# Expert 0's up weights in two column halves with products by contraction, and the remainder's values one group later

## The chip, the cores and the metric

The kernel runs on one core of a Trainium2 chip. The metric is the device time of one launch in microseconds; most launches of this kernel fall between 533.9 and 535.5 us, so that differences under about 1 us can't be read from single times.

## The reference, cut to what matters

Eight batches of retention (causal attention with decay instead of softmax) feed a mixture of four experts that all run on every token.

```
scores = scale * q @ k^T;  ret = scores * Dmat (causal decay)
x      = (ret @ v) as [4608 tokens, 512]
p      = domain_probs / sum(domain_probs)
out    = sum over e of p[:, e] * (relu(x @ w1[e]) @ w2[e])      # w1 512 x 1024, w2 1024 x 512, e = 0..3
```

## The kernel before

One batch has 576 rows: four chunks of 128 and a remainder of 64. Experts work on tiles of 512 tokens. Tile 0 is batch 0's chunks; while its expert products run, the remainder of batch 0 and all of batch 1 are computed in between. The products are cut into *groups* (8 matmuls of 512 columns each for tile 0), and after group n the helper `run(slots, n)` emits whatever was added to slot n. In the traces here, every engine runs its instructions in the order in which they were emitted.

All accumulators of TensorE lie in PSUM and come from one ring of four buffers of two banks each. A new accumulator inherits the buffer of an earlier one, and its first matmul waits until that one has been read.

```python
def load_w1(e, f=slice(0, F)):                      # GpSimd's queue, float32 -> bf16 on the way
    return nc.gpsimd.dma_start(out=w1_sb[e][:, :, f], in_=moe_w1[e][:, f].rearrange("(dc p) f -> p dc f", p=128))

class UpHalf:                                       # expert 0, 512 columns, 256 tokens
    def matmuls(self, i):
        for fc in range(2 * i, 2 * i + 2):          # column block by column block
            for dc in range(NDC):                   # contraction innermost
                nc.tensor.matmul(self.ph[:, fc, :], lhsT=w1_sb[0][:, dc, fc * 128:(fc + 1) * 128],
                                 rhs=xt_of(0)[:, dc, self.c], start=(dc == 0), stop=(dc == NDC - 1))
# ... cuts ...
class Rem:                                          # the remainder of one batch
    def scores(self):
        # ... 4 matmuls into sr ...
        nc.vector.tensor_tensor(self.sT, s, trir[:, :].unsqueeze(1).to_broadcast([128, NP, R]), op=MULT)
    def values(self):
        o = ring_tile("or", [128, NP, R])           # 8 matmuls, 4 of which read sT
# ... cuts ...
load_w1_at = {1: (slice(0, F // 4),), 2: (slice(F // 4, F // 2), slice(F // 2, 3 * F // 4)),
              3: (slice(3 * F // 4, F),)}
# ... cuts ...
for at, f in ((11, lambda: rem0.cast(nc.vector)), (11, rem0.trans_dma), (19, rem0.scores), (20, rem0.values)):
    add(at, f)
for u, (c, tr, sc, o) in enumerate(((18, 21, 22, 23), (20, 22, 24, 25), (24, 0, 28, 29), (25, 0, 29, 30))):
    add(c, lambda u=u: v_cast(u))                   # batch 1: k, q cast on VectorE, v on GpSimd
    if u < 2:
        add(tr, lambda u=u: vs[u].trans_pe())       # pt
    add(o, lambda u=u: vs[u].values())
    add(sc, lambda u=u: v_head(u))                  # s, then kvp
# ... cuts ...
for j, ats in enumerate(((18, 18, 19, 20), (20, 21, 23, 23), (28, 28, 29, 29), (30, 30, 40, 41))):
    for at, which in zip(ats, (3, 1, 2, 4)):        # sums of down weights, on VectorE
        add(at, lambda which=which, j=j: w_sum(which, 4 * j, 4 * j + 4))
```

From group 16 on (expert 2 of tile 0) the order that matters is: four groups of up products, remainder's scores (slot 19), the first group of `po` (down products), the remainder's values (slot 20), the second group of `po`, which two reads of VectorE into `acc` close, `pt` (transposes of batch 1), a group of the next `po`, then `s` (scores), `kvp` (products of keys and values) and another `pt` of batch 1.

Of the kernel before, what the change touches and what calls it, by code (L numbers as in the profile page):

```python
# [23 lines left out]
def kernel(  # L24
# [10 lines left out]
    nc = tc.nc  # L35
    B, H, S, D = q.shape
    N, E = moe_domain_probs.shape
    _, Dm, F = moe_w1.shape
# [7 lines left out]
    NDC = Dm // 128  # L46
# [46 lines left out]
    w1_sb = [const.tile([128, NDC, F], BF16, name=f"w1_{e}") for e in range(E)]  # L93
# [2 lines left out]
    t3w = const.tile([128, KH, HF], BF16, name="t3w")  # L96
    t4w = const.tile([128, KH, HF], BF16, name="t4w")

    def load_w1(e, f=slice(0, F)):
        return nc.gpsimd.dma_start(out=w1_sb[e][:, :, f], in_=moe_w1[e][:, f].rearrange("(dc p) f -> p dc f", p=128))  # L100

    def load_w2(e, lo=0, hi=NFC):
        c = (e % 2) * NFC
# [30 lines left out]
    def warm(n):  # L134
        w = ring_tile("w", [128, 512])
        for _ in range(n):
            nc.tensor.matmul(w, lhsT=zz[:, 0:128], rhs=zz, start=True, stop=True)
# [86 lines left out]
    def xt_of(t):  # L224
        if t not in xt:
            xt[t] = xpool.tile([128, NDC, NT], BF16, tag="xt", name="xt")
        return xt[t]
# [131 lines left out]
    class UpHalf:  # L359
# [4 lines left out]
            self.ph = ring_tile("ph", [128, 4, 256])  # L364

        def matmuls(self, i):
            for fc in range(2 * i, 2 * i + 2):
                for dc in range(NDC):
                    nc.tensor.matmul(self.ph[:, fc, :], lhsT=w1_sb[0][:, dc, fc * 128:(fc + 1) * 128],
                                     rhs=xt_of(0)[:, dc, self.c], start=(dc == 0), stop=(dc == NDC - 1))  # L370

        def relu(self, h):
            nc.scalar.activation(h[:, 0:4, self.c], self.ph, Relu)
# [129 lines left out]
    class Unit:  # L503
# [108 lines left out]
        def values_carried(self):  # L612
# [10 lines left out]
            for g in range(2):  # L623
                p = 2 * self.g + g
                a = 0
                while a < 2:
# [21 lines left out]
    us[0].cast("v", nc.gpsimd)  # L648
    us[0].trans_pe()
    warm(3)  # L650
    load_w1_at = {1: (slice(0, F // 4),), 2: (slice(F // 4, F // 2), slice(F // 2, 3 * F // 4)),
                  3: (slice(3 * F // 4, F),)}
    def cast_unit(u):
        us[u].cast("k", nc.vector)
        us[u].cast("q", nc.vector)
        us[u].cast("v", nc.gpsimd)
        for f in load_w1_at.get(u, ()):
            load_w1(0, f)

    cast_unit(1)  # L660
    us[0].scores()
    warm(4)
# [3 lines left out]
    for u in range(NU):  # L666
        if u + 2 < NU:
            cast_unit(u + 2)
        if u == NU - 1:
            part = UpHalf(0)  # L670
            part.matmuls(0)
        us[u].values_own()
        if u == 2:
            us[3].kv(False, us[2].reads)
        if u + 1 < NU:
            us[u + 1].scores()
        if u == 1:
            us[2].kv(False, us[1].reads)
        us[u].values_carried()
        if u + 2 < NU:  # L680
            us[u + 2].trans_pe(1 - u)
        if u == 0:
            us[1].kv()
            us[2].kvp = us[1].kvt[:, 1]
            us[2].kv_front(us[1].reads)
        if u == 1:
            us[3].kvp = us[1].kvt[:, 0]
            us[3].kv_front(us[2].reads)
# [32 lines left out]
    load_w2(0, NFC // 2, NFC)  # L721
    nc.gpsimd.dma_start(out=p0, in_=moe_domain_probs[0:NT, :].rearrange("(g p) e -> p g e", p=128))
    load_w1(1)
    nc.gpsimd.dma_start(out=prb, in_=moe_domain_probs.rearrange("(p t) e -> p t e", p=128))
    later_tables()
    load_w2(1)
    load_rem(0, nc.gpsimd)
    load_w1(2)
    load_w2(2)
    load_v(0)  # L730
# [12 lines left out]
    add(3, mixing_weights0)  # L743
    add(9, mixing_weights)
    rem0 = Rem(0)
    for at, f in ((11, lambda: rem0.cast(nc.vector)), (11, rem0.trans_dma), (19, rem0.scores), (20, rem0.values)):
        add(at, f)

    def v_cast(u):
# [123 lines left out]
```

## Time and profile before

| | before |
|---|---|
| time, median of 6 in the comparison | 534.39 us (533.86 to 534.95) |
| span of the profiled launch | 532.9 us |
| TensorE busy | 523.0 us, 98% |
| longest wait of TensorE between 18 and 80 us | 0.37 us, at the remainder's values |
| GpSimd's weight loads, expert 0's up weights | 4 of 256 KB |

The busy share says that nearly nothing is to be won anywhere; the list of TensorE's own waits is the view that says what is. Times count from the span's start. KB count bf16, as written; the DMA reads twice as much. The profile can miss some matmul records, so busy time and record count go together (523.0 us with 4212 records here; the program has one matmul for each of the 4251 weight loads).

### The profile page before, as it was taken

The numbers are of one execution on the slowest core, as the hardware profiler recorded it, in microseconds if no ns is written. First come the engines' busy times: TensorE is split into PE (matmuls) and PEld (weight loads), VectorE is DVE, ScalarE is ACT, GpSimd is POOL, SyncE is SP. The second block draws the span as 40 slices with busy tenths as digits, with TensorE's granted clock in tenths as the row PEclk, the third lists the DMA queues.
The fourth block names the chain that finished last, engine by engine and source line by source line (L and its number), as shares of the span: only waits on it lengthen the run. The fifth ranks groups of instructions, "written<-read, shape, count | busy, mean of one in ns | idle before, by whom it ended". The sixth has DMA issues, their size and how long they took to land.

```text
span 532.9 us, 10183 instructions
## 1 busy us (share of the span) xinstructions
PE 523.0 (98%) x4212; PEld 341.4 (64%) x4251; DVE 363.1 (68%) x458; ACT 82.4 (15%) x167; POOL 151.8 (28%) x196
## 2 busy tenths in 40 slices
PE   7999999999999999999999999999999999999997
PEld 3644544478745885478646865587548844884486
DVE  5443968895577667697578767776765567557763
ACT  4722430012101111020101101110110000000010
POOL 5833404245244434235232604162000000000000
PEclk9999999999999999999999999999999999999999
DMA  9999977876769766737353664453010111110001
GB/s 238 181 214 219 244 192 183 171 159 163 153 164 158 169 141 149 162 77 173 95 136 92 149 134 115 104 129 116 20 41 25 56 39 41 41 41 20 1 22 59
DMA packets 146414, 63.74 MB, mean 120 GB/s; under 512 B 124608, under 2 KB 137168, under 8 KB 146368
## 3 DMA queue, kind: packets, MB, share of 16 engines
q1 hardware_dynamic: 134912, 43.61, 35.4%
q0 software_dynamic: 11312, 19.35, 16.9%
q8 instruction: 33, 0.54, 0.4%
q14 instruction: 13, 0.11, 0.1%
q10 hardware_dynamic: 144, 0.13, 0.1%
HBM read 53.56 MB, written 9.51 MB: 118 GB/s over the span
## 4 chain that ended last, share of the span: by engine, by line
PE 73%; ACT 2%; issue 0%; DVE 0%
PE ph L348 36%; PE pd L464 34%; ACT xt L291 2%; PE o L283 1%; PE o L278 1%; PE py L464 1%; DVE h L354 0%; PE or L333 0%; PE or L335 0%; PE sr L327 0%; DVE ob L492 0%
## 5 line engine op out<-in xcount | busy, mean ns | idle before, releaser
L348 PE MATMUL ph<-xt,w 128*128 128x512 bf16 x1103 | 248.6, 379 | 2.5 <-DVE h L354 0.2
L354 DVE SCALAR_TENSOR_TENSOR h<-ph,pB 128x1024 bf16<-128x1024 f32 x128 | 156.5, 1224 | 58.6 <-PE ph L348 57.8
L348 PEld LDWEIGHTS <-w 128*128 128x128 bf16 x1136 | 110.2, 98 | 128.5
L464 PEld LDWEIGHTS <-h 128*128 128x128 bf16 x1024 | 100.0, 98 | 13.3
L464 PEld LDWEIGHTS <-s 128*128 128x128 bf16 x768 | 75.0, 98 | 8.8
L464 PE MATMUL pd<-wx,h 128*128 128x256 bf16 x512 | 61.1, 273 | 0.2
L464 PE MATMUL pd<-wx,s 128*128 128x256 bf16 x512 | 61.1, 273 | 0.0
L219 POOL DMA_DIRECT2D pB<-pd x28 | 15.8, 564 | 154.7 <-DVE h L354 145.6
L499 POOL TENSOR_TENSOR ob<-v,p 128x256 f32<-128x256 f32 x15 | 11.8, 784 | 114.7 <-DVE v L496 86.6
L238 POOL TENSOR_TENSOR bf_k<-raw_k,gk 128x512 bf16<-128x512 f32 x24 | 26.1, 1088 | 36.0 <-DMA raw_k<-in_k_dram 16.3
L270 DVE TENSOR_TENSOR sT<-s,tri 128x1024 bf16<-128x1024 f32 x24 | 28.2, 1219 | 6.3 <-PE s L268 6.3
L437 DVE TENSOR_TENSOR s<-s,h 128x1024 bf16<-128x1024 bf16 x32 | 31.5, 1025 | 0.0
L291 ACT ACTIVATE xt<-o 128x768 bf16<-128x768 f32 (+6 forms) x24 | 13.0, 596 | 116.8 <-PE o L283 116.8
L464 PE MATMUL pd<-t4w,h 128*128 128x256 bf16 x256 | 30.6, 273 | 0.0
L387 PE MATMUL po<-wx,h 128*128 128x512 bf16 x123 | 28.7, 379 | 0.4 <-issue 0.2
L464 PE MATMUL pd<-t2w,s 128*128 128x256 bf16 x240 | 28.7, 273 | 0.0
L464 PE MATMUL pd<-t3w,h 128*128 128x256 bf16 x240 | 28.6, 273 | 0.0
L238 POOL TENSOR_TENSOR bf_q<-raw_q,gq 128x512 bf16<-128x512 f32 x24 | 27.0, 1125 | 4.2 <-DMA rawr_v<-in_v_dram 2.2
L472 ACT ACTIVATE p<-pd 128x256 f32<-128x256 f32 x16 | 6.2, 385 | 138.4 <-PE pd L464 106.2
L435 DVE TENSOR_TENSOR s<-h 128x1024 bf16<-128x1024 bf16 x32 | 24.3, 800 | 0.0
L441 DVE TENSOR_TENSOR s<-h,s 128x1024 bf16<-128x1024 bf16 x32 | 24.3, 800 | 0.0
L481 DVE TENSOR_TENSOR u<-pd,p 128x256 f32<-128x256 f32 x15 | 6.4, 425 | 22.3 <-PE pd L464 22.3
(155 smaller groups left out, 376.0 us busy)
## 6 DMA issues: line engine op xcount, KB each, us to landing
pB<-pd POOLq DMA_DIRECT2D x28, 256.0 KB, 3.6
raw_k<-in_k_dram SPq DMA_DIRECT2D x48, 128.0 KB, 2.9
raw_q<-in_q_dram SPq DMA_DIRECT2D x48, 128.0 KB, 3.0
raw_v<-in_v_dram SPq DMA_DIRECT2D x48, 128.0 KB, 3.1
out_dram<-oa SPq DMA_DIRECT2D x16, 256.0 KB, 2.2
out_dram<-ob SPq DMA_DIRECT2D x15, 256.0 KB, 2.2
w<-in_moe_w_dram POOLq DMA_DIRECT2D x3, 1024.0 KB, 13.5
wx<-in_moe_w_dram POOLq DMA_DIRECT2D x3, 1024.0 KB, 14.7
```

Source lines behind the costliest of these rows:

```text
L219: eng.dma_start(out=pB[t, e], in_=pd[e:e + 1, t * NT:(t + 1) * NT].to_broadcast([128, NT]))
L238: eng.tensor_tensor(bfs[p % 2][n], raw1[n], g[:, :, 2 * p:2 * p + 2].unsqueeze(3).to_broadcast([128, NC, 2, D]), op=MULT)
L270: nc.vector.tensor_tensor(sT[:, :, :, :].rearrange("p j c t -> p (j c) t"), s[:, :, :, :].rearrange("p j c t -> p (j c) t"), tri[:, :].uns ...
L291: nc.scalar.activation(xt_of(t)[:, self.ps, n0 + a - t * NT:n0 + z - t * NT], o[:, :, a:z], Copy)
L348: nc.tensor.matmul(ph[:, f, :], lhsT=w1_sb[e][:, dc, fc * 128:(fc + 1) * 128], rhs=x[:, dc, :], start=(dc == 0), stop=(dc == NDC - 1))
L354: nc.vector.scalar_tensor_tensor(h[:, fk:fk + 2, :], ph, 0.0, pB[t, e][:, :].unsqueeze(1).to_broadcast([128, 2, NT]), op0=MAX, op1=MULT)
L387: nc.tensor.matmul(po[:, gg, :], lhsT=h[:, e * NFC + fc, (2 * m + gg) * 128:(2 * m + gg + 1) * 128], rhs=wx[e // 2][:, (e % 2) * NFC + fc, ...
L435: nc.vector.tensor_tensor(self.alloc("s1")[:, l], h[:, l, self.b], h[:, r, self.b], op=ADD)
L437: nc.vector.tensor_tensor(self.alloc("s2")[:, l], self.s1[:, l], h[:, l, self.a], op=SUB)
L441: nc.vector.tensor_tensor(self.alloc("s4")[:, l], h[:, r, self.a], self.s2[:, l], op=SUB)
L464: mm = nc.tensor.matmul(dst, lhsT=src[:, kk, tok], rhs=rhs(c), start=(start and c == 0), stop=(c == KH - 1), skip_group_check=True)
L499: nc.gpsimd.tensor_tensor(self.ob[:, HF:Dm], self.v, self.p5, op=ADD)
```

## The change

Its intent: expert 0's first products wait for less (the first load brings half of the contraction for 512 columns, so products can start on it); the loads get wider pieces and one issue fewer; and the remainder's values, which waited for VectorE, come one group later, when their operand is ready.

```diff
-    def load_w1(e, f=slice(0, F)):
-        return nc.gpsimd.dma_start(out=w1_sb[e][:, :, f], in_=moe_w1[e][:, f].rearrange("(dc p) f -> p dc f", p=128))
+    def load_w1(e, f=slice(0, F), lo=0, hi=NDC):
+        return nc.gpsimd.dma_start(out=w1_sb[e][:, lo:hi, f],
+                                   in_=moe_w1[e][lo * 128:hi * 128, f].rearrange("(dc p) f -> p dc f", p=128))
@@ class UpHalf
-            for fc in range(2 * i, 2 * i + 2):
-                for dc in range(NDC):
+            for dc in range(2 * i, 2 * i + 2):
+                for fc in range(4):
                     nc.tensor.matmul(self.ph[:, fc, :], lhsT=w1_sb[0][:, dc, fc * 128:(fc + 1) * 128],
-                                     rhs=xt_of(0)[:, dc, self.c], start=(dc == 0), stop=(dc == NDC - 1))
+                                     rhs=xt_of(0)[:, dc, self.c], start=(dc == 0 and fc % 2 == 0),
+                                     stop=(dc == NDC - 1), skip_group_check=True)
@@ loads
-    load_w1_at = {1: (slice(0, F // 4),), 2: (slice(F // 4, F // 2), slice(F // 2, 3 * F // 4)),
-                  3: (slice(3 * F // 4, F),)}
+    half = [slice(0, F // 2), slice(F // 2, F)]
+    load_w1_at = {1: ((half[0], 0, 2),), 2: ((half[0], 2, 4), (half[1], 0, 4))}
-            load_w1(0, f)
+            load_w1(0, *f)
@@ slots
-(19, rem0.scores), (20, rem0.values)):
+(19, rem0.scores), (21, rem0.values)):
```

Because a line is added near the top and two further down, line numbers after the change are one or two higher than before: the values are L333 before and L334 after, `kvp` L564 and L566, `acc` L399 and L401, t3w L408 and L410.

More of the change, by code (lines that the diff above doesn't have):

```diff
@@ L745 @@
     rem0 = Rem(0)
-    for at, f in ((11, lambda: rem0.cast(nc.vector)), (11, rem0.trans_dma), (19, rem0.scores), (20, rem0.values)):
+    for at, f in ((11, lambda: rem0.cast(nc.vector)), (11, rem0.trans_dma), (19, rem0.scores), (21, rem0.values)):
         add(at, f)
```

## The prediction

> **What bounds the kernel now.** I read the page's busy shares and slices first, to see whether any stage leaves TensorE idle; then the stretches of the first 60 us, where all three edits lie; then TensorE's own waits; then the ordered timeline around the one wait that an edit touches.
>
> ```profile
> PE 523.0 (98%) x4212; PEld 341.4 (64%) x4251; DVE 363.1 (68%) x458; ACT 82.4 (15%) x167; POOL 151.8 (28%) x196
> ...
> PE   7999999999999999999999999999999999999997
> ```
>
> TensorE is busy 98% of a 532.9 us span; only the first slice (filling) and the last (draining) show idle time. The number and width of its matmuls set the time, and a change that keeps them all can only recover waits.
>
> ```profile
> 10.00:17.40 7.40, 7.07 (x157) 5.11 (x158) 6.21 (x10) 5.89 (x13) 5.72 (x9) 1.00 1.19 214
> 17.40:22.00 4.60, 4.46 (x56) 3.67 (x55) 2.20 (x15) 2.90 (x6) 4.22 (x13) 1.00 1.20 172
> 22.00:29.00 7.00, 6.96 (x33) 3.17 (x33) 1.49 (x11) 3.81 (x7) 4.90 (x8) 1.00 1.19 210
> 32.20:60.00 27.80, 27.27 (x157) 12.76 (x159) 15.16 (x25) 9.61 (x10) 13.82 (x18) 1.00 1.15 223
> ```
>
> Columns: stretch, its length, busy us of TensorE, weight loads, VectorE, ScalarE and GpSimd, then clock, DMA share, GB/s. Where expert 0's products run (17.4 to 29) TensorE idles 0.14 + 0.04 us. From 32.2 to 60 it idles 0.53 us. DMA is saturated throughout, yet TensorE, which consumes the weights, is not waiting for them.
>
> ```profile
> PE or L333 <- DVE sTr L328: 0.4, 1, 0.4
> ```
>
> This is nearly all of that 0.53 us, and the only wait of TensorE that an edit aims at: the remainder's values wait for VectorE's masked scores. The timeline shows why they are late:
>
> ```profile
> 51.97 0.69 DVE L516 TENSOR_TENSOR bf_k<-raw_k,gk 128x512 bf16<-128x512 f32 x1 [4.36 <-DMA raw_k<-in_k_dram]
> ...
> 53.02 1.89 PE L387 MATMUL po<-wx,h 128*128 128x512 bf16 x7
> ...
> 54.81 0.42 DVE L328 TENSOR_TENSOR sTr<-sr,trir 128x256 bf16<-128x256 f32 x1
> ...
> 55.28 0.19 PE L333 MATMUL or<-sTr,bfr_v 128*128 128x64 bf16 x1 [0.37 <-DVE sTr L328]
> ...
> 55.51 1.89 PE L387 MATMUL po<-wx,h 128*128 128x512 bf16 x8
> ...
> 58.85 1.40 DVE L399 SCALAR_TENSOR_TENSOR acc<-po,pm,acc 128x512 f32<-128x512 f32 x2
> ...
> 59.85 0.72 PE L564 MATMUL kvp<-bf_v,bf_k 128*128 128x128 bf16 x8
> ```
>
> VectorE stood 4.36 us for batch 1's first k load, and then worked without a pause from 52.87 to 60.25. The mask at 54.81 is one place in that late queue.
>
> **What the Trainium skill says.** (1) "PSUM — Partial Sum Buffer", The four PSUM rules: two accumulation groups open in one bank may not both use the first-matmul flag, because it clears the whole bank's written bits; flagging only the first matmul issued in the bank works. With contraction outermost, two 256-column groups are open in each 2 KiB bank, and the diff flags only the even one. No run of before shows it (there each group closes before the next opens). (2) "TensorE: Matmul & The Clock Gate", Back-to-back issue gap: N/2.4 + 2.5 ns for an isolated matmul, so 109 ns at N = 256. The trace agrees: 24 of them last 2.78 us, and (2.78 - 0.27)/23 = 109 ns. Its sustained 131 ns at N = 512 is not seen: 31 steps in 7.07 us less one 0.38 give 216 ns. The measurement decides. (3) "DMA: Bandwidth & Descriptors", Why small descriptors are slow: a fixed cost per packet. The trace agrees: by its packet records the GpSimd queue finishes about 155 KB/us (bf16 side) in 512 B pieces from 18 to 20 us, and about 200 KB/us in 1024 B pieces from 21 to 24 us.
>
> **The change part by part.**
>
> *Loads.* Four loads of 256 columns, all contractions (4 x 256 KB), become A (512 columns, contraction 0 and 1, 256 KB), B (512 columns, 2 and 3, 256 KB) and the second half (512 KB). Removed: one issue on GpSimd, 0.74 us at 15.28, so every later issue can go 0.7 us sooner. The pieces double from 512 B to 1024 B: 1024 KB at 155 is 6.6 us, at 200 it is 5.1 us, so I estimate that the queue, saturated from here to 55 us, runs **1.5 us earlier** afterwards. What that is worth on TensorE: in before the four quarters land at issue plus landing time, 10.08 + 5.7 = 15.8, then 18.2, 19.7 and 21.1; they are first read at 17.4, 19.2, 21.8 and 23.6. Expert 1's up weights land at 18.23 + 13.5 = 31.7 and are read at 31.97. All arrive in time, by 0.2 to 2.5 us. So **0** in the profiled run; perhaps 0.1 to 0.2 us in runs where that 0.2 us margin fails.
>
> *First products by contraction.* 32 matmuls of 256 columns before and after, in another order, with as many weight loads: 32 x 0.109 us both ways. Second-half tokens no longer need contraction 2 and 3 (the last unit's rows, written by ScalarE until 20.17) for their first 8 matmuls; but those start at about 20.07 and the whole run of 24 is already at 109 ns, so the gain is at most 0.05 us. **0.**
>
> *Values one group on.* In before, TensorE goes from the last of 8 products (start 54.53, 8 x 0.216 from 53.02) to the values at 55.28; after, the next 8 products follow at 54.75. So 55.28 - 54.75 = **0.53 us** saved (0.37 idle plus the modelled tail of the last matmul). The 8 values matmuls still cost 55.51 - 55.28 = 0.23 us, one group later, where their mask is 1.7 us old.
>
> *A moved buffer.* The built order shows one side effect that the diff doesn't tell. The values' accumulator is now taken after the first `po` pair is closed, so the free accumulators queue up otherwise: batch 1's first `kvp` takes the buffer that `po` had, where in before the second `pt` took it. Its first weight load waits for VectorE in the after program and not in before. The last read of `po` is the pair at 58.85, ending 60.25. After, TensorE reaches `kvp` at 59.85 - 0.53 = 59.32. If VectorE is not earlier, that is a wait of 60.25 - 59.32 = 0.93 us, of which the 0.53 us won would be lost and 0.4 us more. If the loads come 1.5 us sooner, k lands at 50.4, VectorE's run of 7.4 us from the q cast (52.87 to 60.25) starts at 51.4 and ends near 58.8 to 59.1, delayed a little by the mask, which can't run before the scores at 53.2. So no wait, with 0.2 to 0.5 us to spare.
>
> Sum: -0.53 (values) - 0.1 (margins) + 0 = about -0.6 us on 534.44: **533.8 us**.
>
> **The rivals.** *The new buffer wait eats the gain.* For it: the chain above is tight; VectorE's length varies (one mask product takes 1.09 us in place of 0.69 beside a GpSimd cast). Against it: the load shift. It makes 534.0 to 534.8. *The wider loads shift nothing.* For it: the first quarters landed 1.4 us apart for 256 KB, about the rate at which the later 1024 B loads landed, so the packet rates may overstate the gain. Then VectorE stays late and the rival before comes true: 534.8. *Earlier loads free more than I count.* If unprofiled runs do wait for weights whose margins are 0.2 us (expert 1's up weights, the second half of expert 0's down weights, which land at 26.77 for a read at 27.0), the shift removes that too: 533.0 to 533.4. Against it: the three times, 533.86 to 534.95, lie close to the profiled run's 534.68, which has no such wait. *The second half of expert 0's up weights comes too late,* as one 512 KB load in place of two: it is read at 21.8, and in before its two quarters had landed by 21.1 with more issue work ahead of them, so I don't believe it; it would cost up to 0.5 us.
>
> **Range and chances.** All effects found lie between -1.5 and +0.9 us. The three runs of before spread by 1.1 us. Together, 8 in 10: 532.9 to 534.8. Two per cent is 10.7 us; TensorE has about 10 us of idle time in all, most of it at the ends. So within 2% is nearly sure.
>
> **What would show it.** Right: the 0.37 us wait at the values is gone, the values run after 16 unbroken products; expert 0's up weights are all landed by about 19.6; expert 1's land near 30.2; VectorE's stall for k falls from 4.36 to about 2.9 us; `kvp` starts without a wait on VectorE; busy time of TensorE stays 523 us. Wrong: `kvp` or its weight load waiting for `acc`, or landings unmoved. The prediction fails as a whole only if the loads delay TensorE at 17.4 or 21.8, or if timed runs wait for weights where the profiled one did not.

## The result, and the profile after

The changed kernel took 534.77 us (median of 6, 534.40 to 535.71) against 534.39 us. The ratio is 1.0008, 95% interval 0.9996 to 1.0021. Ratios here are the mean time of one kernel's fast runs over that of the other's of the same rounds, so not quite the ratio of the medians. By time alone the two kernels are the same. The predicted gain of 0.6 us is not there; the launches profiled are 532.9 us before and 533.3 us after.

To see more than the noise of whole launches shows, I cut each trace at four matmuls of TensorE that all kernels have: expert 0's first product, the remainder's scores of batch 0, the first values of batch 1, and the next remainder's scores.

| stretch on TensorE, us | before | after |
|---|---|---|
| start to expert 0's first product | 17.45 | 17.35 |
| to the remainder's scores | 35.45 | 35.45 |
| to batch 1's first values | 9.89 | 10.37 |
| to the next remainder's scores | 30.46 | 30.46 |
| to the end | 439.70 | 439.70 |

Four of five agree to 0.1 us or better. The second, which holds all of expert 0's products and the landing of its last up weights, is equal. The whole difference is in the third, 0.48 us, where the values were moved.

The same stretches as in the prediction, of the changed kernel (length, busy us of TensorE, weight loads, VectorE, ScalarE, GpSimd, then clock, DMA share, GB/s):

```profile
17.40:22.00 4.60, 4.47 (x57) 3.64 (x54) 2.31 (x17) 2.87 (x7) 4.21 (x14) 1.00 1.16 187
22.00:29.00 7.00, 7.00 (x34) 3.15 (x33) 1.24 (x7) 3.72 (x7) 4.02 (x6) 1.00 1.14 199
32.20:60.00 27.80, 27.09 (x157) 12.52 (x154) 15.48 (x25) 9.59 (x10) 13.10 (x17) 1.00 1.16 217
```

The loads arrive in time as before, and where expert 0 starts TensorE has the same 0.1 us to lose. From 32.2 to 60 it is idle 0.71 us in place of 0.53. The list of TensorE's waits names the place (engine and line, what was waited for: us in total, times, longest):

```profile
PE kvp L566 <- DVE acc L401: 1.0, 1, 1.0
```

The wait at the values is gone from that list and this one is new. The timeline of the changed kernel around it (start us, us, engine, line, operation, tiles):

```profile
51.47 0.69 DVE L518 TENSOR_TENSOR bf_k<-raw_k,gk 128x512 bf16<-128x512 f32 x1 [3.97 <-DMA raw_k<-in_k_dram]
52.38 0.69 DVE L518 TENSOR_TENSOR bf_q<-raw_q,gq 128x512 bf16<-128x512 f32 x1 [0.21 <-DMA raw_q<-in_q_dram]
...
52.92 3.62 PE L389 MATMUL po<-wx,h 128*128 128x512 bf16 x16
...
54.31 0.42 DVE L329 TENSOR_TENSOR sTr<-sr,trir 128x256 bf16<-128x256 f32 x1
...
56.37 0.19 PE L334 MATMUL or<-sTr,bfr_v 128*128 128x64 bf16 x1
...
56.76 1.09 DVE L416 TENSOR_TENSOR t4w<-wx,t2w 128x1024 bf16<-128x1024 bf16 x1
...
57.26 1.05 POOL L516 CAST bf_v<-rx 128x512 bf16<-128x512 f32 x1
57.77 1.09 DVE L410 TENSOR_TENSOR t3w<-wx,wx 128x1024 bf16<-128x1024 bf16 x1
58.79 1.40 DVE L401 SCALAR_TENSOR_TENSOR acc<-po,pm,acc 128x512 f32<-128x512 f32 x2
58.87 0.26 PEld L552 LDWEIGHTS <-qkT 64*64 64x64 bf16 x16 [0.42 <-issue]
...
60.24 0.72 PE L566 MATMUL kvp<-bf_v,bf_k 128*128 128x128 bf16 x8 [0.95 <-DVE acc L401]
```

The third edit did what it was meant to do: `po` runs as 16 products in one piece and the values follow without a wait. But `s` at 58.87 ends at 59.22 and `kvp` starts at 60.24: TensorE stands 1.02 us until VectorE has read `po`, whose buffer `kvp` now inherits. VectorE got its k 0.50 us sooner (51.47, was 51.97), and yet finished reading `po` at 60.19, where before it was 60.25. For comparison, the same three records in the kernel before:

```profile
57.24 0.68 DVE L414 TENSOR_TENSOR t4w<-wx,t2w 128x1024 bf16<-128x1024 bf16 x1
...
57.84 1.09 DVE L408 TENSOR_TENSOR t3w<-wx,wx 128x1024 bf16<-128x1024 bf16 x1
...
58.27 1.13 POOL L514 CAST bf_v<-rx 128x512 bf16<-128x512 f32 x1
```

Before, GpSimd's cast lay beside one weight sum of VectorE; after, having started 1.0 us sooner, it lies beside two, and each takes 1.09 us where it takes 0.68 us alone (an experiment below tests that the cast is the cause). So 0.41 us of the 0.50 us that the loads won is lost again on VectorE.

TensorE's busy time reads 525.0 us after and 523.0 us before, which is no change: the after trace has all 4251 matmul records, the one before 39 fewer.

```profile
PE 525.0 (98%) x4251; PEld 341.2 (64%) x4251; DVE 362.8 (68%) x458; ACT 82.2 (15%) x167; POOL 151.5 (28%) x195
```

### The profile page after: what moved, and what is told of

Read it like the earlier page. It is cut to its first block, busy times and chain, and to the rows that moved or that the text cites. A ratio compares the mean times of both kernels' runs of the same rounds, so it can differ in the third digit from the quotient of the medians.

```text
span 533.3 us, 10221 instructions
## 1 busy us (share of the span) xinstructions
PE 525.0 (98%) x4251; PEld 341.2 (64%) x4251; DVE 362.8 (68%) x458; ACT 82.2 (15%) x167; POOL 151.5 (28%) x195
## 4 chain that ended last, share of the span: by engine, by line
PE 73%; ACT 2%; DVE 0%; issue 0%
PE ph L349 37%; PE pd L466 34%; ACT xt L292 2%; PE o L284 1%; PE o L279 1%; PE py L466 1%; DVE h L355 0%; PE or L334 0%; PE sr L328 0%; PE or L336 0%; DVE ob L494 0%
## 5 line engine op out<-in xcount | busy, mean ns | idle before, releaser
L439 DVE TENSOR_TENSOR s<-s,h 128x1024 bf16<-128x1024 bf16 x32 | 29.5, 961 | 0.0
```

The lines of the kernel that those rows point to most:

```text
L439: nc.vector.tensor_tensor(self.alloc("s2")[:, l], self.s1[:, l], h[:, l, self.a], op=SUB)
```

## The experiments

**The theory:** the moved values make `kvp` inherit `po`'s buffer, and so TensorE waits for VectorE's read of `po`; how long depends on when batch 1's k lands and on the order of VectorE's work. **Rivals:** the new loads or the new product order cost something themselves; `kvp` waits for something else; it was one unlucky profile. All twelve runs gave right results. I also looked in the built programs at the places of the buffers: `kvp` lies where `po` lay in the changed kernel and in e2, e3, e4, e6, e8 and e9; in the kernel before, e1 and e5 the second `pt` does.

The table at the end of this section has every run. "Lateness of k" is the start of the k cast on VectorE (it starts as soon as k lands) less the start of expert 0's first product; "run" is VectorE's time from the start of the q cast to the last read of `po`; "wait" is TensorE's wait at `kvp` (start less that of `s`, less the 0.35 us that `s` takes until the next matmul can start, as from 59.51 to 59.85 in the kernel before), and "stretch" goes from the remainder's scores to batch 1's first values. 9.35 us is its length without any wait.

### The loads without the move, and the move without the loads

```diff
 e1_loads: the changed kernel with
-(21, rem0.values)
+(20, rem0.values)
 e2_values: the kernel before with
-(20, rem0.values)
+(21, rem0.values)
```

> The change without its third edit (values stay one group earlier; loads and product order changed). Theory (the changed kernel loses through the buffer wait that the moved values bring): kvp takes the buffer it had in the kernel before and does not wait; the values wait less than 0.37 us because VectorE is some 0.5 us earlier (0.0 to 0.2 us left); 0.3 to 0.5 us under the kernel before, about 534.0. Rival (the new loads cost something themselves): as slow as the changed kernel, 534.8.

> The third edit alone on the kernel before (values one group on; old loads, old product order). Theory: the 0.37 us wait at the values goes, kvp waits 0.9 to 1.1 us for the last read of po by VectorE (acc), so the time is 0.4 to 0.6 us over the kernel before, 534.8 to 535.0. Rival (the wait of kvp comes from the changed loads' timing): no wait, 0.5 us under the kernel before, 533.9.

Loads and order alone: 0.9995 (0.9979 to 1.0011), no wait at the values or at `kvp`, stretch 9.41 us. The move alone: 0.9996 (0.9979 to 1.0013), and the wait at `kvp` is back, with the old loads, in the list of waits and in the timeline:

```profile
PE kvp L564 <- DVE acc L399: 1.3, 1, 1.3
```

```profile
58.35 1.57 DVE L408 TENSOR_TENSOR t3w<-wx,wx 128x1024 bf16<-128x1024 bf16 x1
58.75 0.62 POOL L514 CAST bf_v<-rx 128x512 bf16<-128x512 f32 x1
59.85 1.40 DVE L399 SCALAR_TENSOR_TENSOR acc<-po,pm,acc 128x512 f32<-128x512 f32 x2
```

Its stretch is 10.71 us, the longest of all. So the move brings the wait, without the new loads and the new product order, and these two do not bring it without the move. (In this launch GpSimd's cast lay within one weight sum; the cast kept its 0.62 us and the sum alone took 0.89 us longer.) The times can't confirm this: the expected +0.4 us or more of the second kernel is not in its ratio; the first kernel's ratio is 0.3 us under before, as expected; but both intervals are over 3 tenths of a per cent wide, some 1.7 us, and hold either answer. Here the trace decides.

### VectorE's order changed, so that `po` is read sooner

```diff
 both: the changed kernel, the second tuple of weight sums
-(20, 21, 23, 23)
+(21, 21, 23, 23)     e4_one_sum_later
+(22, 22, 23, 23)     e3_sums_later
```

> The changed kernel with one weight sum (t3w of the second quarter, 1.09 us on VectorE, just ahead of the last read of po) emitted one group later, so that VectorE reads po 1.0 us sooner; nothing else moves. Theory: kvp's wait of 0.95 us goes to 0.0 to 0.1 us and the time falls by 0.9 us against the changed kernel, to about 0.5 us under the kernel before, 533.8 to 534.0. Rival (kvp's wait only hides a later one on the same chain, say for the mask of the scores): the wait reappears within the next 5 us and the time stays at 534.6 to 534.8.

> The changed kernel with two weight sums (t3w and the wx difference of the second quarter, 1.09 and 0.68 us) emitted two groups later, behind the scores' mask and the carry. Theory: kvp does not wait, and the mask and carry come earlier as well, so the 0.2 us wait of the values on the state at about 63 us can't appear; 533.7 to 534.0. Rival: the sums now delay the accumulate at 63 us and its buffer's next user, and a wait of 0.3 to 0.7 us moves there; 534.3 to 534.6.

With one sum (t3w) behind the read of `po`, the wait is gone and the stretch is 9.35 us, 1.02 us under the changed kernel's. In its timeline the read ends at 58.64, and `kvp` follows `s` directly:

```profile
57.24 1.40 DVE L401 SCALAR_TENSOR_TENSOR acc<-po,pm,acc 128x512 f32<-128x512 f32 x2
58.57 0.67 DVE L410 TENSOR_TENSOR t3w<-wx,wx 128x1024 bf16<-128x1024 bf16 x1
58.94 0.42 PE L552 MATMUL s<-qkT 64*64 64x128 bf16 x16
...
59.29 0.72 PE L566 MATMUL kvp<-bf_v,bf_k 128*128 128x128 bf16 x8
```

The ratio to the kernel before is 0.9996 (0.9978 to 1.0015). With both sums two groups later the stretch is 9.35 us as well, but a new wait of 0.2 us appears further on, for a transpose that starts later because VectorE's next cast does; the stretch after it grows from 30.46 to 30.73 us. Its ratio is 0.9986 (0.9971 to 1.0001). The wait of 0.2 us for the state, which the changed kernel has at 81.4 us (the expectation puts it at 63), is gone. The rival was half right here: work that is pushed back does come out somewhere, though not at the accumulate that I had named.

### The wait goes with the buffer

Emitting one more weight sum ahead of the read makes the build exchange the buffers: `pt` inherits `po`'s, and `kvp` does not.

```diff
 e5_swapped_buffers: the changed kernel, the second tuple of weight sums
-(20, 21, 23, 23)
+(20, 20, 23, 23)
```

> The changed kernel with one more weight sum (0.68 us on VectorE) emitted ahead of the last read of po; in the build kvp and the following pt then exchange buffers, so that pt, and not kvp, inherits po's buffer. Theory (the wait belongs to whoever inherits po's buffer): kvp does not wait; pt, which TensorE reaches 0.66 us later, waits about 1.0 us, for VectorE is 0.68 us later too; from the remainder's scores to the first values of batch 1 it takes 10.4 us as in the changed kernel (10.37). Rival (kvp waits for something else that ends at 60.2): kvp still waits 1 us and pt another 0.6; 11.0 us or more.

`kvp` did not wait, and `pt` did:

```profile
PE pt L529 <- DVE acc L401: 0.2, 1, 0.2
```

The place is as expected; the size is not (0.2 us against about 1.0), since in this launch k's lateness was 33.28 us and not 34.12: VectorE was 0.84 us sooner, which is the missing part. The ratio is 1.0019 (0.9994 to 1.0044), which the trace does not explain, its stretch being 9.58 us.

### GpSimd's cast taken away from VectorE's sums

```diff
 e8_cast_scalar: the changed kernel
-        vs[u].cast("v", nc.gpsimd)
+        vs[u].cast("v", nc.scalar if u == 1 else nc.gpsimd)     # with a Copy activation in cast()
```

> The changed kernel with one cast (batch 1's second v, 1.05 us on GpSimd at 57.26) on ScalarE. Theory (the earlier loads were given back because that GpSimd cast now lies beside two bf16 sums of VectorE, 1.09 us each in place of 0.68): both sums take 0.68 us, VectorE's run from the q cast to the last read of po shrinks from 7.8 to 7.0 us, kvp's wait from 0.95 to 0.1 to 0.2 us, the stretch from remainder's scores to the values of batch 1 from 10.37 to 9.5 us. Rival (the sums take 1.09 us for another reason, such as DMA writes to the same memory): they stay at 1.09 and kvp's wait stays near 0.95.

Both sums now take 0.68 us and VectorE's run is 6.96 us, 0.85 less than in the changed kernel:

```profile
56.81 0.68 DVE L416 TENSOR_TENSOR t4w<-wx,t2w 128x1024 bf16<-128x1024 bf16 x1
57.42 0.68 DVE L410 TENSOR_TENSOR t3w<-wx,wx 128x1024 bf16<-128x1024 bf16 x1
58.02 1.39 DVE L401 SCALAR_TENSOR_TENSOR acc<-po,pm,acc 128x512 f32<-128x512 f32 x2
...
59.47 0.72 PE L569 MATMUL kvp<-bf_v,bf_k 128*128 128x128 bf16 x8 [0.36 <-DVE acc L401]
```

The wait is 0.43 us, not the 0.1 to 0.2 expected, because k came 0.25 us later than in the first profile of the changed kernel. Ratio 0.9990 (0.9975 to 1.0005). That the GpSimd cast stretches the sums is shown, and with it where the 0.43 us come from by which VectorE's run was longer than before (7.81 against 7.38): one sum was stretched there, two after.

### The old product order with the new loads, and a narrower second half

```diff
 e6_columns_first: the changed kernel, UpHalf as in the kernel before
 e7_narrow_half: the changed kernel
-    load_w1_at = {..., 2: ((half[0], 2, 4), (half[1], 0, 4))}
+    load_w1_at = {..., 2: ((half[0], 2, 4), (slice(F // 2, 3 * F // 4), 0, 4), (slice(3 * F // 4, F), 0, 4))}
```

> The changed kernel with expert 0's first products column by column again (old order, new loads): the first 8 then need the second contraction piece at 17.35, where it lands at 17.6. Theory (the order is worth nothing by itself, it only lets the first 8 start on the first piece): TensorE waits 0.2 to 0.3 us there, but it waits until 18.5 for the mask anyway, so from the first product to the remainder's scores it takes 35.45 us as in both kernels, at most 35.55. Rival (the order saves something): 35.7 or more.

> The changed kernel with the second column half loaded as two loads of 256 columns (512 B pieces, one issue more). Theory (part of the shift of the loads comes from the wider pieces and part from the issue saved): expert 0's last up weights land 0.6 to 0.9 us later than in the changed kernel, batch 1's first k 0.3 to 0.7 us later, and kvp's wait grows by as much, up to 0.5 us. Rival (the shift is chance from run to run): the landings, counted from the first product, scatter within 0.4 us of the changed kernel's.

With the old order, expert 0's first product to the remainder's scores takes 35.45 us, as everywhere but in e2. The expected wait for the second piece did not even occur: it landed at 16.89, and the first product began at 17.01. So the order is worth nothing in time in this launch; what it is worth when that piece lands late (at 17.59, 0.24 us after the first product, in the first profile of the changed kernel) was not tested. The ratio, 1.0015 (0.9997 to 1.0033), is not clear of noise, and the stretch of 9.85 us doesn't explain it.

The narrow half is inconclusive. Expert 0's last up weights landed 3.3 us after the first product (2.8 and 2.5 in the changed kernel, 2.3 to 4.2 over all runs with the new loads) and k at 34.11 us, equal to the changed kernel's first profile and inside what the other new-load runs show. `kvp`'s wait was 1.00 us, the stretch 10.35. The ratio, 1.0017 (1.0002 to 1.0032), is the only one whose interval leaves out 1; its 0.9 us are twice what its stretch has over that of before (10.35 against 9.89), and the rest is not explained.

### The two kernels again, and the order of VectorE's work without the loads

```diff
 e9_no_loads: the kernel before with two numbers changed
-(20, rem0.values)        -(20, 21, 23, 23)
+(21, rem0.values)        +(21, 21, 23, 23)
```

> The kernel before once more, for a second profile of its loads. Theory (kvp's and the values' waits follow from when k of batch 1 lands, counted from expert 0's first product): k lands 34.3 to 34.8 us after it (34.49 in the first profile, 34.59 in the run with the values alone), and from the remainder's scores to batch 1's first values it takes 9.9 us. Rival (landings of the old loads scatter as widely as those of the new, 33.3 to 34.3): a value under 34.1 says that the shift of the loads is mostly chance.

> The changed kernel once more. Theory: kvp's wait is k's landing after the first product less 33.15 us (0.95 at 34.10; 0.43 at 33.59 in the run with the old product order): with k at 33.3 to 34.3 the wait is 0.2 to 1.1 us, and the stretch from the remainder's scores to batch 1's first values 9.6 to 10.5 us. Rival (the wait does not depend on the loads): 0.95 us again whatever k does.

> The kernel before with the values one group on and one weight sum one group later; old loads, old product order. Theory (the order of VectorE's work decides, the loads are a bonus): VectorE reads po 1.09 us sooner, at most 59.2, just ahead of kvp; kvp waits 0.0 to 0.3 us and the stretch from remainder's scores to batch 1's first values takes 9.35 to 9.65 us, 0.25 to 0.55 under the kernel before. Rival (the new loads are needed): kvp waits 0.5 us or more, 9.9 us as in the kernel before.

> The changed kernel with one weight sum one group later, again, on the chip of the two kernels it is compared with. Theory: no wait of kvp whatever the loads do, 9.35 us from the remainder's scores to batch 1's first values, 0.5 us under the kernel before and 0.3 to 1.0 us under the changed one. Rival (the first profile was a lucky one): a wait of 0.3 us or more.

The kernel before, profiled again, **has no wait at its values**: k came at 33.91 and the mask was done before the products:

```profile
51.14 0.69 DVE L516 TENSOR_TENSOR bf_k<-raw_k,gk 128x512 bf16<-128x512 f32 x1 [3.75 <-DMA raw_k<-in_k_dram]
...
53.98 0.42 DVE L328 TENSOR_TENSOR sTr<-sr,trir 128x256 bf16<-128x256 f32 x1
...
54.52 0.19 PE L333 MATMUL or<-sTr,bfr_v 128*128 128x64 bf16 x1
```

Its stretch is 9.35 us, the floor, so the wait that the third edit removes is there in one profile and absent in the other; the expectation of 9.9 us was wrong, and k under 34.1 speaks for the rival that loads scatter. The changed kernel again had k at 34.50, and a wait of 1.35 us, exactly what the line through the earlier points says (34.50 - 33.15):

```profile
51.54 0.69 DVE L518 TENSOR_TENSOR bf_k<-raw_k,gk 128x512 bf16<-128x512 f32 x1 [4.34 <-DMA raw_k<-in_k_dram]
...
60.26 0.72 PE L566 MATMUL kvp<-bf_v,bf_k 128*128 128x128 bf16 x8 [1.28 <-DVE acc L401]
```

Two numbers changed in the old kernel, with the old loads, give 9.35 us though k came late, at 34.50; the read of `po` started at 57.94 and ended at 59.33, `kvp` at 59.44:

```profile
57.33 0.68 DVE L414 TENSOR_TENSOR t4w<-wx,t2w 128x1024 bf16<-128x1024 bf16 x1
57.94 1.39 DVE L399 SCALAR_TENSOR_TENSOR acc<-po,pm,acc 128x512 f32<-128x512 f32 x2
58.41 0.62 POOL L514 CAST bf_v<-rx 128x512 bf16<-128x512 f32 x1
59.26 0.68 DVE L408 TENSOR_TENSOR t3w<-wx,wx 128x1024 bf16<-128x1024 bf16 x1
```

The cast now lies beside the read of `po` and takes 0.62 us, and the sums 0.68. The repeat of the one-sum kernel has 9.35 us too.

| kernel | loads | ratio to before (95%) | lateness of k | VectorE's run | wait at kvp | stretch |
|---|---|---|---|---|---|---|
| before | old | - | 34.52 | 7.38 | 0 (values: 0.54) | 9.89 |
| r_before | old | 0.9995 (0.9972 to 1.0018) | 33.91 | 7.39 | 0 | 9.35 |
| e2_values | old | 0.9996 (0.9979 to 1.0013) | 34.61 | 7.88 | 1.36 | 10.71 |
| e9_no_loads | old | 0.9986 (0.9966 to 1.0007) | 34.50 | 6.38 | 0 | 9.35 |
| after | new | 1.0008 (0.9996 to 1.0021) | 34.12 | 7.81 | 1.02 | 10.37 |
| r_after | new | 1.0012 (0.9978 to 1.0046) | 34.50 | 7.79 | 1.35 | 10.70 |
| e1_loads | new | 0.9995 (0.9979 to 1.0011) | 33.83 | 7.81 | 0 (pt: 0.06) | 9.41 |
| e4_one_sum_later | new | 0.9996 (0.9978 to 1.0015) | 33.55 | 6.80 | 0 | 9.35 |
| r_one_sum_later | new | 1.0004 (0.9978 to 1.0030) | 33.48 | 6.77 | 0 | 9.35 |
| e3_sums_later | new | 0.9986 (0.9971 to 1.0001) | 33.48 | 6.79 | 0 | 9.35 |
| e5_swapped_buffers | new | 1.0019 (0.9994 to 1.0044) | 33.28 | 8.53 | 0 (pt: 0.2) | 9.58 |
| e6_columns_first | new | 1.0015 (0.9997 to 1.0033) | 33.62 | 7.81 | 0.50 | 9.85 |
| e8_cast_scalar | new | 0.9990 (0.9975 to 1.0005) | 34.37 | 6.96 | 0.43 | 9.78 |
| e7_narrow_half | mixed | 1.0017 (1.0002 to 1.0032) | 34.11 | 7.78 | 1.00 | 10.35 |

What follows: in the four launches with the changed kernel's order of work (after, r_after, e6, e7) the wait at `kvp` is the lateness of k less 33.10 to 33.15 us, whatever the wait is. The kernel before starts to wait, by its one launch that waits, only at 34.52 - 0.54 = 33.98; the other, at 33.91, doesn't wait. So the change made TensorE sensitive to loads that come 0.86 us sooner than it had to mind before. With one weight sum behind the read of `po`, it does not wait at 34.50 (e9).

No version beats both kernels by more than the timing can show: the best stretch is 0.54 us, 0.1%, under that of the first profile of before, and equal to that of the second. That waits of this size make the launches of one kernel slower than those of another is thus read from the traces; no ratio here shows it.

## Why the prediction was wrong, point by point

**The values' gain, -0.53 us: right.** The 0.37 us wait is gone, and the stretch without any wait is 9.35 us, 0.54 under 9.89. What the prediction did not see is that the kernel before also reaches 9.35 when k is early.

**Expert 0's products by contraction, 0: right.** 35.45 us from the first product to the remainder's scores in both kernels and with the old order. As the Trainium skill's page "PSUM — Partial Sum Buffer", The four PSUM rules, says, two groups open in a bank work when only the first matmul issued in it has the flag: results were right in every run with this order.

**The margins of weights, -0.1 us: too small to see.** Neither profile of before has such a wait. One launch with the old loads (e2) has two, 0.08 us at 19.67 and 0.15 at 27.63, and its second stretch is 35.68 us in place of 35.45; none with the new loads has. So one launch in four with the old loads had something for the new loads to win, 0.23 us.

**The moved buffer: the mechanism right, the verdict wrong.** The prediction named the chain (`kvp` takes `po`'s buffer, waits for `acc`, loses what was won and 0.4 us more) and then chose "So no wait, with 0.2 to 0.5 us to spare". The trace has the wait of 1.02 us and a stretch 0.48 us longer. This is the step that failed, and what came in its place is the prediction's own first rival, "The new buffer wait eats the gain" (534.0 to 534.8 there; 534.77 measured). Two of its terms were mis-sized:

- *"If the loads come 1.5 us sooner"*: they came 0.50 us sooner in the two launches compared (51.47 against 51.97; 0.40 counted from expert 0's first product). The other signs say the same: expert 0's last up weights landed at 20.14 us (predicted 19.6; 21.08 before), expert 1's at 31.11 (30.2; 31.76 before), and VectorE stood 3.97 us for k (2.9; 4.36 before). Over all launches of the table but the mixed one, lateness is 34.39 on average with the old loads (four, 33.91 to 34.61) and 33.80 with the new (nine, 33.28 to 34.50): 0.6 us, between two groups that overlap. (From the span's start it is 51.9 and 51.0 us, but there TensorE's first product is 0.3 us sooner too.) The 1.5 us came from 1024 KB at 155 and at 200 KB/us, each read from a few microseconds of one launch. Over 15 to 19 us in the packet records of all those launches GpSimd's queue finishes 161 KB/us in 512 B pieces (138 to 181) and 178 in 1024 B pieces (159 to 185), so 1024/161 - 1024/178 = 0.6 us. The rates overlap too, so the agreement with the skill's cost per packet that the prediction read from one launch is weaker than it looked. The rival "the wider loads shift nothing" was nearer. How much of the 0.6 is the piece width and how much the issue saved stays open, since the one kernel that would tell them apart lies within the scatter.
- *"VectorE's run of 7.4 us from the q cast"*: it took 7.81. I took the run as fixed, while moving VectorE and GpSimd, and GpSimd's cast came to lie beside two sums (0.41 us each) and not one. Taking the cast away gave the time back. The prediction had the number (1.09 in place of 0.69) among the rivals, where it calls the weight sum t3w a mask product, and did not put it into the sum.

1.5 - 0.5 for the loads and 0.4 for the run make 1.4 us, which turns the predicted end of the read, 58.8, into the measured 60.2.

**The range.** It reached to 534.8 on the slow side, which just holds the median; the mean ratio makes it 534.4 x 1.0008 = 534.8. The predicted centre is 1 us below. That "within 2% is nearly sure" was right and says little on a kernel of which TensorE fills 98%. The "about 10 us" of idle time behind it counts the 39 missing matmul records as idle; the trace after, which misses none, has 533.3 - 525.0 = 8.3 us.

## What to carry to other kernels

Moving one accumulator by a group changes who inherits whose buffer. Before believing a gain, list for each accumulator that follows in the ring whose last read it now waits for, and when that read ends. Where such a margin is a few tenths of a microsecond, take the input's arrival from several launches: here the wait grew one for one with the landing of a load that scatters by 1.2 us. And an engine that gets its input sooner does not finish sooner by as much; look at what the other engines then do beside it.

## What the Trainium skill lacked or had wrong

- "DMA: Bandwidth & Descriptors", Why small descriptors are slow: says that small packets have a fixed cost, but gives no rates for casting loads by piece size. Measured here (float32 to bf16, on GpSimd's queue, bf16 side): 161 KB/us on average in 512 B pieces and 178 in 1024 B pieces, with 138 to 185 from launch to launch.
- "SBUF — State Buffer", Who interferes with whom: says that a VectorE instruction with two SBUF inputs contends with a GpSimd instruction that reads SBUF. The trace agrees: a bf16 sum takes 1.09 us beside GpSimd's cast and 0.68 without it. The page gives no size for this. In the changed kernel a cast cost two sums 0.82 us together and itself took 1.05 us; in e2 the sum alone lost (1.57 us) and the cast took 0.62, so who loses how much differed between these two launches.
- "TensorE: Matmul & The Clock Gate", Back-to-back issue gap: its sustained 131 ns for 512 columns is not seen; 216 ns in every stretch here, which is the page's isolated figure.
- No page has how far the landing of one and the same load scatters between launches: counted from the first product, 0.6 us between two launches of the kernel before, 0.4 between two of the changed one, and over all kernels with the same loads 0.7 (old) and 1.2 us (new), enough to make a wait of 0.54 us come and go.
